# One-DMA loads for q, k and a, a removed pair of tiles, and 28 unread products behind TensorE's first fillers, in a fused gated-attention and feed-forward kernel

## The chip, the cores and the metric

The kernel runs on one core of a Trainium2 chip. The metric is the device time of one execution in microseconds (us). Before the change, three runs took 514.45, 516.45 and 517.21 us, with a median of 516.45 us. Lower is better.

A core has five engines that run side by side and wait for each other by semaphores: TensorE (PE, matrix products; its weight loads are shown apart as PEld), VectorE (DVE), ScalarE (ACT), GpSimd (POOL) and SyncE (SP), which here only issues DMAs. SBUF is the on-chip memory with 128 rows, PSUM the accumulator of TensorE.

## The reference

A gated linear recurrence for 4 batches of 8 heads, 768 tokens, 48 values a head, followed by a feed-forward block with an ELU on 3072 tokens:

```
for t in range(S):
    state = alpha[:, :, t, :, None] * state + np.einsum('bhd,bhe->bhde', k[:, :, t], v[:, :, t])
    y[:, :, t] = np.einsum('bhd,bhde->bhe', q[:, :, t], state)
...
h = x @ w_in                                          # 3072x384 by 384x2048
g = np.where(h > 0.0, h, np.exp(np.minimum(h, 0.0)) - 1.0)
return g @ w_out                                      # 3072x2048 by 2048x384
```

## The kernel before

The work falls into a recurrence part and a feed-forward part, in one stream of instructions for each engine.

**Recurrence.** The 768 tokens of each batch are cut into 6 chunks of 128 tokens, so there are 24 chunks, numbered i. (The title of the code's list is `win`; here they are called chunks, since "window" is a view of the profile.) Heads go in pairs: a pair has one head in rows 0 to 47 of SBUF and the other in rows 64 to 111; rows 48 to 63 and 112 to 127 are padding. For each chunk, `SC` takes running products of a (alpha) on VectorE, `LN` and `EX` take logarithm and exponential on ScalarE, `KA`, `KB`, `KC` and `SQ` scale k and q by them, `TP` transposes k on TensorE and `KN` copies the result (later chunks do it in `TA`, `TB` and `T` on VectorE), `S` makes the scores k by q, `MK` masks them, `U` makes k by v, `UP`, `UA`, `UB` and `UC` carry the state on, and `YL`, `Y3`, `Y`, `XH`, `XP` and `XL` make the output y and split it into a rounded upper and a remaining lower part, the input of the feed-forward part.

**Feed-forward.** 3072 tokens are 12 blocks of 256, and the 2048 hidden values are 8 slices of 256. For block b and slice j, `A` is 18 products of 128x256 (h), `RA`, `RB`, `RC`, `GH` and `GL` apply the ELU and split it, and `O` is 12 products of 128x384. The weights come as 16 loads of 768 KB (`F.0` to `F.15`); `DA`, `DB` and `DC` on VectorE, `WH` on ScalarE and `WP` or `WL` on TensorE, ScalarE, GpSimd or VectorE turn them into the upper and lower parts that TensorE uses.

**Order.** Each engine's order is written out by hand: the text `START` lists steps as name and number (`L.3` is step `L` for chunk 3), and `STEADY` does the same for the rest. Every step issues its instructions in that order, on whatever engines it uses, and each engine takes its own in order. All loads before the last block go through one queue, SP's. In the part that matters here the order on SP is

```
LA.0 LA.1 LB.0 LB.1 F.0 F.2 LV.0 LV.1 LV.2 L.2 L.3 F.4 F.6 LV.3 F.12 F.3 F.1 F.7 L.4 LV.5 F.5 L.5 F.11 F.10 F.9 F.14 LV.4 F.8 L.7 L.6
```

`LV` loads v. `LA` and `LB` load a and then k and q of chunks 0 and 1, over all 128 rows. `L` (line 178) loads all three of a later chunk into one of `NQ` = 3 tiles `qka`: for chunk 2 in one DMA over 128 rows (770 KB), and from chunk 3 on in two DMAs of 48 rows (289 KB each), without the padding rows. A load of chunk i has to wait until the last reader of chunk i - 3 is done with the tile; for `L.3` that is `S.0`.

**The head of the program.** `first` is a constant of 1e-30 with ones in some places, set by VectorE. As soon as it is there, TensorE runs `X(WARM)`: 12 products of 128x512 on it, read as bf16 and written to the PSUM tile `wp`, which nobody reads. They are here called the fillers. Next on TensorE stands `TP.0` (line 285), which waits for `KC.0` on VectorE (line 244). GpSimd meanwhile sets constants and clears parts of the v tiles (line 135) and two tiles `v0` (line 139); step `V0`, which would load them, stands in no list, and `U` reads them in no chunk.

Of the kernel before, what the change touches and what calls it, by code (L numbers as in the profile page):

```python
# [8 lines left out]
F32 = mybir.dt.float32  # L9
F32R = mybir.dt.float32r  # L10
# [4 lines left out]
B, H, S, D = 4, 8, 768, 48  # L15
# [11 lines left out]
QW = 2 * NP * W + NP * AW  # L27
# [3 lines left out]
EARLY = 6  # L31
# [3 lines left out]
QU, QS = 6, 6  # L35
# [53 lines left out]
def gla_elu_ffn(ctx: ExitStack, tc: tile.TileContext, qka, vv, vn, wgt, out):  # L89
    nc = tc.nc  # L90

    const = ctx.enter_context(tc.tile_pool(name="const", bufs=1))
    weights = ctx.enter_context(tc.tile_pool(name="weights", bufs=1))
    main = ctx.enter_context(ExitStack())
    work = main.enter_context(tc.tile_pool(name="work", bufs=2))
# [10 lines left out]
    for a in range(2):  # L106
        nc.vector.tensor_copy(out=sel[64 * a:64 * a + 64, a, :, D:64],
                              in_=ident[64 * a:64 * a + 64, 64 * a:64 * a + D].rearrange("p (x c) -> p c x", c=NC))
# [4 lines left out]
    for h0 in (0, 64):  # L113

        nc.gpsimd.affine_select(
            out=mask[h0:h0 + 64, :], in_=mask[h0:h0 + 64, :], pattern=[[1, C]],
            compare_op=ALU.is_ge, fill=0.0, base=0, channel_multiplier=-1)
    first = const.tile([128, NP, AW], F32, name="first")
    nc.vector.memset(first, 1e-30)
    nc.vector.memset(first[:, :, 0:1], 1.0)  # L120
    wp = psa.tile([128, 512], F32, name="wp", tag="pa")
    wz = first.rearrange("p n w -> p (n w)").bitcast(mybir.dt.bfloat16)

    def X(n):
        for _ in range(n):
            nc.tensor.matmul(wp, lhsT=wz[:, 0:128], rhs=wz[:, 0:512], start=True, stop=True)

    X(WARM)

    NB = 4  # L130

    HD = 2 * NP * D
    vs_t = [work.tile([128, 3 * HD + 16], F32, name=f"vs{i}", tag=f"vs{i}", bufs=1) for i in range(NB)]
    for t in vs_t:
        nc.gpsimd.memset(t[:, 2 * HD:], 0.0)

    v0 = [work.tile([128, HD], F32, name=f"v0{i}", tag=f"v0{i}", bufs=1) for i in range(2)]
    for t in v0:
        nc.gpsimd.memset(t, 0.0)

    def lhs(i, c, a):

# [23 lines left out]
    NQ = 3  # L166
    qka_t = [work.tile([128, QW], F32, name=f"qka{i}", tag=f"qka{i}", bufs=1) for i in range(NQ)]

    def qtile(i):
        t = win[i]["t"] = qka_t[i % NQ]  # L170
        return t


    @tok
    def L(i):
        t = qtile(i)
        for r in [slice(0, 128)] if i < NQ else [slice(0, D), slice(64, 64 + D)]:
            nc.sync.dma_start(out=t[r], in_=qka[i, r, 0:QW])

    @tok  # L180
    def LA(i):
# [14 lines left out]
            nc.sync.dma_start(out=vs[0:64, 0:2 * HD], in_=vv[i, 0:64])  # L196
            nc.sync.dma_start(out=vs[64:128, HD:3 * HD], in_=vv[i, 64:128])


    @tok  # L200
    def V0(i):
        if EARLY <= i < QU:
            nc.sync.dma_start(out=v0[i % 2][0:64], in_=vv[i, 0:64, HD:2 * HD])

    @tok
    def SC(i):
# [548 lines left out]
    start = [t.split(".") for t in START.split()]  # L755
# [215 lines left out]
```

## Time and profile before

| | before |
|---|---|
| runs | 514.45, 516.45, 517.21 us (median 516.45) |
| profiled execution, span | 516.5 us |
| PE busy | 501.1 us (97%) |
| DVE busy | 391.1 us (76%) |
| ACT busy | 288.9 us (56%) |
| POOL busy | 127.9 us (25%) |
| DMA queue of SP | 55.69 MB, 38.0% of 16 engines' span |
| mean granted TensorE clock | 0.978 |

The span runs from the first to the last instruction of the profiled execution; it has no other time beside it, and it agrees with the median of the runs. Idle time of an engine is shown in front of the instruction that ended it, with the one that released it ("<-"). The granted clock (PEclk) is a share of TensorE's full speed. The DMA share is the mean busy share of the 16 DMA engines.

### The profile page before, as it was taken

To read this page: it belongs to the slowest core of one execution; us is meant where nothing else is said; L and a number is where in the kernel's file an instruction comes from. 1 tells how busy PE (TensorE), PEld (TensorE's weight loads), DVE (VectorE), ACT (ScalarE), POOL (GpSimd) and SP (SyncE) were. 2 spreads that over 40 slices of the span, in tenths; PEclk is the share of its full clock that TensorE was granted. 3 is DMA by queue.
4 is the path that set the end of the run, shared out by engine and by line. 5 is a ranking of instruction groups with operands and counts; after the bars stand their busy time and mean duration, and the time that the engine had idled before them with its cause. 6 is when DMAs were issued, how large, how long until landed. Compare 5 with 4: busy or idle time off the path is not lost.

```text
span 516.5 us, 13313 instructions
## 1 busy us (share of the span) xinstructions
PE 501.1 (97%) x5400; PEld 484.2 (94%) x5400; DVE 391.1 (76%) x808; ACT 288.9 (56%) x689; POOL 127.9 (25%) x110
## 2 busy tenths in 40 slices
PE   5998999998999999999999999999999999999995
PEld 2887999997999999999999999999999999999995
DVE  7886999997989878886986987886987987244321
ACT  3463667544564366755755655756655656454432
POOL 2020855463213300501511511501501500000000
PEclk8698999998999999999999999999999999999999
DMA  8999724217221426326326326326323321210001
GB/s 303 322 314 313 210 58 155 75 41 161 67 75 27 68 94 162 93 72 160 97 73 160 92 79 154 93 83 148 94 87 99 93 66 44 62 39 10 2 32 36
DMA packets 22069, 57.00 MB, mean 110 GB/s; under 512 B 3217, under 2 KB 10129, under 8 KB 22001
## 3 DMA queue, kind: packets, MB, share of 16 engines
q1 hardware_dynamic: 21712, 55.69, 38.0%
q8 instruction: 44, 0.72, 0.6%
q10 hardware_dynamic: 288, 0.39, 0.2%
q14 instruction: 25, 0.20, 0.1%
HBM read 49.39 MB, written 4.72 MB: 105 GB/s over the span
## 4 chain that ended last, share of the span: by engine, by line
PE 85%; DMA 6%; DVE 4%; issue 2%; POOL 1%; ACT 1%; SPq 0%; DVEq 0%; POOLq 0%
PE o L709 39%; PE h L658 37%; DMA qka<-in_qka_dram 4%; PE y L461 4%; DMA raw<-in_wgt_dram 2%; PE q L377 2%; PE q L333 2%; PE y L456 1%; DVE st L361 1%; PE sc L349 1%; DVE P L212 0%; DVE kn L295 0%; DVE spare L596 0%; DVE spare L590 0%; DVE h L676 0%
## 5 line engine op out<-in xcount | busy, mean ns | idle before, releaser
L658 PE MATMUL h<-xt,w 128*128 128x256 f32 x1728 | 217.3, 283 | 1.9 <-DVE st L361 1.9
L658 PEld LDWEIGHTS h<-xt,w 128*128 128x128 f32 x1728 | 211.3, 190 | 4.0 <-issue 2.2
L709 PE MATMUL o<-w,gh 128*128 128x384 f32 x768 | 199.1, 340 | 0.0
L709 PEld LDWEIGHTS o<-w,gh 128*128 128x128 f32 x768 | 136.9, 188 | 0.8
L709 PE MATMUL o<-w,gl 128*128 128x384 f32 x384 | 130.0, 339 | 0.1
L682 ACT CAST gh<-h 128x512 fp32r<-128x512 f32 x96 | 56.0, 583 | 81.2 <-DVE h L676 44.4
L695 DVE TENSOR_TENSOR gl<-h,gh 128x512 fp32r<-128x512 f32 x96 | 65.9, 687 | 36.7 <-ACT gh L682 35.2
L295 DVE STREAM_TRANSPOSE kn<-qka 32x128 f32<-32x128 f32 x288 | 87.1, 303 | 4.5
L666 ACT ACTIVATE r<-h 128x512 f32<-128x512 f32 x96 | 56.9, 596 | 55.0 <-PE h L658 52.2
L676 DVE SCALAR_TENSOR_TENSOR h<-r,h 128x512 f32<-128x512 f32 x96 | 64.4, 688 | 15.4 <-ACT r L671 14.6
L709 PEld LDWEIGHTS o<-w,gl 128*128 128x128 f32 x384 | 72.1, 188 | 0.4 <-DVE gl L695 0.4
L234 POOL TENSOR_TENSOR qka<-qka,R 128x512 f32<-128x512 f32 x19 | 24.6, 1295 | 192.9 <-DVE gl L695 117.2
L671 ACT ACTIVATE r<-r 128x512 f32<-128x512 f32 x96 | 59.1, 632 | 0.6
L264 POOL TENSOR_TENSOR st<-qka,P 64x512 f32<-64x512 f32 x36 | 43.6, 1211 | 15.1 <-DVE P L212 13.3
L361 DVE TENSOR_TENSOR st<-q,mask 64x256 f32<-64x256 f32 x72 | 30.4, 422 | 10.8 <-ACT vs L412 9.2
L212 DVE TENSOR_TENSOR_SCAN P<-qka,first 128x516 f32<-128x516 f32 x24 | 30.2, 1264 | 3.4 <-DMA qka<-in_qka_dram 3.0
L239 POOL TENSOR_TENSOR R<-P,R 128x512 f32<-128x512 f32 x20 | 25.1, 1257 | 11.2 <-DVE qka L234 9.8
L221 ACT ACTIVATE R<-P 128x512 f32<-128x512 f32 x24 | 15.2, 633 | 22.6 <-DVE P L212 22.6
L414 DVE TENSOR_TENSOR vs<-vs,q 48x192 f32<-48x192 f32 x30 | 10.5, 349 | 21.3 <-PE q L333 17.0
L514 ACT ACTIVATE y<-y 128x128 fp32r<-128x128 f32 x20 | 5.6, 278 | 29.7 <-PE y L461 27.5
L642 POOL TENSOR_TENSOR w<-spare,w 128x768 fp32r<-128x768 f32 x6 | 16.0, 2674 | 19.7 <-ACT w L622 19.6
L614 ACT ACTIVATE ck<-ck,lim 128x384 f32<-128x384 f32 x32 | 20.7, 646 | 0.1
(102 smaller groups left out, 438.5 us busy)
## 6 DMA issues: line engine op xcount, KB each, us to landing
raw<-in_wgt_dram SPq DMA_DIRECT2D x16, 768.0 KB, 13.1
ck<-in_wgt_dram SPq DMA_DIRECT2D x32, 384.0 KB, 3.1
qka<-in_qka_dram SPq DMA_DIRECT2D x42, 288.8 KB, 6.8
vs<-in_vv_dram SPq DMA_DIRECT2D x36, 192.0 KB, 3.9
out_dram<-ot SPq DMA_DIRECT2D x22, 192.0 KB, 1.9
vs<-in_vv_dram SPq DMA_DIRECT2D x6, 384.0 KB, 11.9
xt<-y SPq DMA_DIRECT2D x40, 48.0 KB, 2.3
qka<-in_qka_dram SPq DMA_DIRECT2D x2, 512.0 KB, 6.2
```

The costliest lines, as they stand in the source:

```text
L212: nc.vector.tensor_tensor_scan(out=P.rearrange("p n w -> p (n w)"), data0=t[:, 2 * NP * W:], data1=first.rearrange("p n w -> p (n w)"), in ...
L239: eng(KBV, i).tensor_tensor(out=d["R"], in0=pw(i), in1=d["R"], op=ALU.mult)
L264: eng(SQV, i).tensor_tensor(out=st[r, a], in0=d["q"][r], in1=pw(i)[r], op=ALU.mult)
L295: nc.vector.transpose(out=kn[32 * t:32 * t + 32, :, 32 * g:32 * g + 32], in_=d["kt"][32 * g:32 * g + 32, :, 32 * t:32 * t + 32])
L361: nc.vector.tensor_tensor(out=d["st"][r, a, :, c * C:(c + 1) * C], in0=d["s4"][a][o], in1=mask[o].unsqueeze(1).broadcast_to([64, NP, C]), ...
L658: nc.tensor.matmul(h[:, f, :], lhsT=t[:, wi, ws], rhs=x[:, c, xi, :], start=(f == 0 and k == 0), stop=(k == 8), skip_group_check=True)
L666: nc.scalar.activation(out=r, in_=d["h"], func=AF.Relu, scale=-1.0)
L671: nc.scalar.activation(out=d["r"], in_=d["r"], func=AF.Exp, scale=-1.0)
L676: nc.vector.scalar_tensor_tensor(out=d["h"], in0=d["r"], scalar=-1.0, in1=d["h"], op0=ALU.add, op1=ALU.max)
L682: nc.scalar.copy(out=gh, in_=d["h"])
L695: nc.vector.tensor_tensor(out=gl, in0=d["h"], in1=d["gh"].bitcast(F32), op=ALU.subtract)
L709: nc.tensor.matmul(o[:, 0:DM], lhsT=gt[:, f, ms], rhs=t[:, wi, f * DM:f * DM + DM], start=(j == 0 and f == 0 and k == 0), stop=(j == NJ - ...
```

## The change

Three edits. The first removes the two `v0` tiles, their two clears on GpSimd and the step that was never called. The second makes `L` one DMA over all 128 rows for every chunk, so the padding rows are loaded too. The third adds, behind the fillers, a constant `fr` (a copy of 512 columns of `first` on ScalarE, rounded to fp32r) and 28 products into `wp`, which nobody reads: 17 of 256 columns in fp32r (5 and 4 plain ones, 4 whose moving operand repeats one column, 4 over 64 rows), 8 of 256 columns in bf16, and 3 of 512 columns in fp32r.

```diff
     X(WARM)
+    fr = const.tile([128, 512], F32R, name="fr")
+    nc.scalar.copy(out=fr, in_=first.rearrange("p n w -> p (n w)")[:, 0:512])
+
+    def probe(n, w, lhs, rhs, start):
+        for _ in range(n):
+            nc.tensor.matmul(wp[:, 0:w], lhsT=lhs, rhs=rhs, start=start, stop=True, skip_group_check=True)
+
+    probe(5, 256, fr[:, 0:128], fr[:, 0:256], True)
+    probe(4, 256, fr[:, 0:128], fr[:, 0:256], False)
+    probe(4, 256, wz[:, 0:128], wz[:, 0:256], False)
+    probe(4, 256, wz[:, 0:128], wz[:, 0:256], True)
+    probe(4, 256, fr[:, 0:128], fr[:, 0:1].broadcast_to([128, 256]), False)
+    probe(4, 256, fr[0:64, 0:128], fr[0:64, 0:256], False)
+    probe(3, 512, fr[:, 0:128], fr[:, 0:512], False)
...
-    v0 = [work.tile([128, HD], F32, name=f"v0{i}", tag=f"v0{i}", bufs=1) for i in range(2)]
-    for t in v0:
-        nc.gpsimd.memset(t, 0.0)
...
     def L(i):
         t = qtile(i)
-        for r in [slice(0, 128)] if i < NQ else [slice(0, D), slice(64, 64 + D)]:
-            nc.sync.dma_start(out=t[r], in_=qka[i, r, 0:QW])
+        nc.sync.dma_start(out=t, in_=qka[i, :, 0:QW])
...
-    @tok
-    def V0(i):
-        if EARLY <= i < QU:
-            nc.sync.dma_start(out=v0[i % 2][0:64], in_=vv[i, 0:64, HD:2 * HD])
```

The order changes at two places. The first is TensorE's, at the end of the fillers (`wp` from `first`) and the start of chunk 0 (`tp`, `sc`). Before:

```order
L126 LDWEIGHTS first
L126 MATMUL wp<-first 128x512
L285 MATMUL tp<-ident,qka_123 128x128 x4
L349 MATMUL sc<-st,qka_123 64x64 x16
L285 MATMUL tp<-ident,qka_124 128x128 x4
```

With the change (of eight like pairs on `first`, one is shown):

```order
L126 LDWEIGHTS first
L126 MATMUL wp<-first 128x512
L134 MATMUL wp<-fr 128x256 x9
L134 LDWEIGHTS first
L134 MATMUL wp<-first 128x256
...
L134 MATMUL wp<-fr 128x256 x8
L134 MATMUL wp<-fr 128x512 x3
L289 MATMUL tp<-ident,qka_149 128x128 x4
L353 MATMUL sc<-st,qka_149 64x64 x16
```

So 28 products now stand between the last filler and the transposes of chunk 0; nothing else on TensorE moves.

The second place is SP's queue from `L.2` (the first row) to `L.4`; `qka` are the tiles of the loads in question, `raw` weights, `vs` v. Before:

```order
L178 DMA qka_125<-in_qka_dram 128x1540
L178 DMA qka_123<-in_qka_dram 48x1540 x2
L568 DMA raw_235<-in_wgt_dram 128x1536 x2
L194 DMA vs_108<-in_vv_dram 128x768
L568 DMA raw_294<-in_wgt_dram 128x1536
L568 DMA raw_328<-in_wgt_dram 128x1536 x2
L568 DMA raw_378<-in_wgt_dram 128x1536
L178 DMA qka_124<-in_qka_dram 48x1540 x2
```

With the change:

```order
L187 DMA qka_151<-in_qka_dram 128x1540
L187 DMA qka_149<-in_qka_dram 128x1540
L572 DMA raw_260<-in_wgt_dram 128x1536 x2
L203 DMA vs_138<-in_vv_dram 128x768
L572 DMA raw_319<-in_wgt_dram 128x1536
L572 DMA raw_353<-in_wgt_dram 128x1536 x2
L572 DMA raw_403<-in_wgt_dram 128x1536
L187 DMA qka_150<-in_qka_dram 128x1540
```

The sequence of loads stays; each of the loads of chunk 3 and later is one issue of 128 rows in place of two of 48.

## The prediction

> **What bounds the kernel now.** I read the page's engine lines first, then TensorE's waits, then stretches of the first 54 us, and last single rows of them.
>
> ```profile
> PE 501.1 (97%) x5400; PEld 484.2 (94%) x5400; DVE 391.1 (76%) x808; ACT 288.9 (56%) x689; POOL 127.9 (25%) x110
> PEclk8698999998999999999999999999999999999999
> DMA  8999724217221426326326326326323321210001
> ```
>
> TensorE is busy for 501.1 of 516.5 us, so an edit counts only if it removes TensorE's idle time or lets it run faster. The other two lines give each fortieth of the span: the clock is low in the second slice (12.9 to 25.8 us), and the DMA engines are full in the first four.
>
> ```profile
> PE tp L285 <- DVE qka L244: 3.6, 1, 3.6
> PE yl L456 <- DVE vs L414: 2.1, 1, 2.1
> PE h L658 <- DVE st L361: 1.9, 1, 1.9
> ```
>
> These are TensorE's waits (us in total, times, longest) apart from 2.1 us at the very start: one behind the fillers, one near 45 us, one near 123 us. The next view gives stretches: start and end, length, busy time (and count) of PE, PEld, DVE, ACT and POOL, then granted clock, DMA share and GB/s.
>
> ```profile
> 6.24:9.66 3.42, 0.49 (x3) 0.00 (x0) 1.99 (x4) 1.25 (x4) 0.00 (x0) 0.95 1.01 392
> 9.66:13.07 3.41, 2.71 (x36) 2.41 (x36) 3.34 (x6) 0.72 (x2) 0.00 (x0) 0.50 1.01 414
> 13.07:16.48 3.41, 3.41 (x48) 2.84 (x44) 3.34 (x3) 1.68 (x5) 0.00 (x0) 0.50 1.09 378
> 16.48:19.90 3.42, 3.42 (x60) 3.15 (x60) 1.74 (x3) 1.05 (x2) 0.00 (x0) 0.50 1.00 184
> 19.90:23.31 3.41, 3.41 (x18) 2.73 (x16) 3.12 (x5) 0.85 (x2) 1.18 (x1) 0.55 0.99 338
> 23.31:26.72 3.41, 3.41 (x71) 2.64 (x71) 2.46 (x4) 2.48 (x8) 0.00 (x0) 1.00 1.01 407
> 43.79:47.20 3.41, 1.26 (x17) 1.06 (x15) 2.29 (x4) 0.60 (x1) 0.00 (x0) 0.95 0.98 288
> 47.20:50.61 3.41, 3.41 (x54) 2.96 (x53) 3.38 (x3) 1.61 (x4) 0.00 (x0) 0.54 1.00 399
> ```
>
> Each of the waits is followed by half clock. TensorE works only 0.49 us of 6.24:9.66, and then runs at 0.50 from 9.66 to about 23.3 us; it works 1.26 us of 43.79:47.20, and runs at half for the next 3.4 us. So from 10.4 to 23.3 us TensorE is "busy" all the time because it is slow.
>
> ```profile
> 8.00:16.00 8.00, 5.64 (x72) 4.89 (x72) 7.83 (x11) 2.29 (x6) 0.00 (x0) 0.58 1.04 408
> 16.00:20.00 4.00, 4.00 (x68) 3.61 (x65) 2.32 (x3) 1.16 (x3) 0.00 (x0) 0.50 1.04 188
> 24.00:32.00 8.00, 8.00 (x150) 6.60 (x148) 6.75 (x9) 5.10 (x15) 0.00 (x0) 1.00 1.03 416
> 34.00:46.00 12.00, 10.64 (x147) 9.81 (x143) 6.87 (x10) 5.93 (x12) 3.86 (x2) 1.00 1.02 238
> 124.00:128.00 4.00, 2.87 (x14) 2.90 (x15) 1.67 (x4) 0.00 (x0) 3.48 (x3) 0.68 1.02 182
> ```
>
> The DMA engines are full in all five, yet move 408 to 416 GB/s in some and 182 to 238 in others. What differs is what is under way, by SP's issues:
>
> ```profile
> 6.04 8.14 SPq L178 DMA_DIRECT2D qka<-in_qka_dram  x3
> 121.85 2.46 SPq L178 DMA_DIRECT2D qka<-in_qka_dram  x4
> ```
>
> The three issues from 6.04 us are `L.2` and the two halves of `L.3`, the last of them about 14.2 us, and 16:20 is slow; behind 34:46 stand the halves of `L.4` and `L.5`; and 124:128 holds hardly anything but the four halves issued from 121.85 us. `L.2`, with rows just as long but 128 of them, lies in the fast 8:16. So the loads of 48 rows halve the rate, of everything beside them too.
>
> **The change, part by part: the probes.** I call the 28 new products probes. They have 25 x 256 + 3 x 512 = 7,936 columns.
>
> ```profile
> 2.08 4.65 PE L126 MATMUL wp<-first 128*128 128x512 bf16 x12 [2.08 <-DVE first L120]
> 10.36 1.08 PE L285 MATMUL tp<-ident,qka 128*128 128x128 f32 x4 [3.63 <-DVE qka L244]
> 4.62 0.15 PEld L126 LDWEIGHTS <-first 128*128 128x128 bf16 x1 [0.27 <-issue]
> 5.04 0.15 PEld L126 LDWEIGHTS <-first 128*128 128x128 bf16 x1 [0.28 <-issue]
> 69.92 2.12 PE h L658 x18
> 72.04 4.24 PE o L709 x24
> ```
>
> The last two are pieces of the chain that ended last: 18 products of 256 columns in 2.12 us (0.118 each), 24 of 384 in 4.24 (0.46 ns a column). At this rate the probes take 25 x 0.118 + 3 x 0.236 = 3.66 us, and the hole from 6.73 to 10.36 us is 3.63. I cost them at 0.03 us, hidden by the wait for `KC.0`. Fillers come every 0.42 us (4.62 to 5.04), 512 columns at half of that rate, although the clock column starts at 1.00; at that rate the probes would take 6.5 us and `TP.0` would be 2.9 us late. The forms that no row shows (a repeated column, 64 rows, adding onto `wp`) I put between these two ends and take the faster, as the nearest row, `h`, is the same fp32r at 256 columns. The copy to `fr` lies on ScalarE, idle from 2.1 to 4.87 us.
>
> What they buy is the clock, if a TensorE that doesn't pause keeps 1.00 beyond 9.66 us. Then the work of 10.4 to 23.3 us shrinks to about half, but what TensorE does there depends on VectorE, which has no gap from 7.6 to 17.4 us. So I add up the waits that fall away on VectorE and ScalarE:
>
> ```profile
> 18.39 0.36 DVE L445 SCALAR_TENSOR_TENSOR vs<-u,P 128x192 f32<-128x192 f32 x1 [1.02 <-PE u L395]
> 19.41 1.23 DVE L212 TENSOR_TENSOR_SCAN P<-qka,first 128x516 f32<-128x516 f32 x1 [0.66 <-DMA qka<-in_qka_dram]
> 22.07 0.36 DVE L445 SCALAR_TENSOR_TENSOR vs<-u,P 128x192 f32<-128x192 f32 x1 [0.25 <-PE u L421]
> 24.77 0.27 ACT L489 COPY y<-yl 128x128 f32<-128x128 f32 x1 [0.70 <-PE yl L456]
> ```
>
> 1.02 and 0.25 (for `U.0` and `UP.1` on TensorE), 0.66 (the landing of `L.2`, whose tail shares 16:20 with `L.3`) and 0.70 (`YL.0`) lie one behind the other on the way to `Y.0`: 2.63 us. `Y.0` starts at 25.13 us now and would start near 22.5; what is late next there is ScalarE's `LN.2` and `EX.2`. TensorE's 13.0 us at half clock would be 6.5 at full, of which 2.6 come out at `Y.0`; the other 3.9 us become holes in front of it.
>
> **The loads.** Of one chunk 591 KB become 788 KB. The next rows say what waits for them.
>
> ```profile
> 40.21 1.23 DVE L212 TENSOR_TENSOR_SCAN P<-qka,first 128x516 f32<-128x516 f32 x1 [1.59 <-DMA qka<-in_qka_dram]
> 44.91 0.96 DVE L584 TENSOR_SCALAR wm<-raw 128x1536 int32<-128x1536 int32 x1 [3.46 <-DMA raw<-in_wgt_dram]
> 46.38 0.35 DVE L414 TENSOR_TENSOR vs<-vs,u 128x192 f32<-128x192 f32 x1
> 46.78 1.11 PE L456 MATMUL yl<-st,vs 48*64 48x64 f32 x16 [2.15 <-DVE vs L414]
> 47.82 1.55 PE L500 MATMUL y<-y,sel 128*64 128x128 f32 x12
> 51.29 0.88 PE L500 MATMUL y<-y,sel 128*64 128x128 f32 x12
> ```
>
> VectorE waits for `L.4`, then for the weights `F.5` that queue behind it; its step at 46.38 us then ends TensorE's wait of 2.15 us. At 408 GB/s, 16:20 would take 4.0 x 188/408 = 1.84 us, and 34 to 44.9 would take 10.9 x 238/408 = 6.4: 6.7 us less. The added padding of `L.3` and `L.4` costs 2 x 197 KB / 408 GB/s = 1.0. `F.5` lands 5.7 us earlier, near 39.2; VectorE is there by then (2.6 us earlier than now, and without the 1.59).
>
> TensorE is without a gap from 25.13 to 44.64 us at clock 1.00, so it brings its 2.6 us to 42.0. The row of 46.38 us comes 5.7 earlier, at 40.7, and the wait of 2.15 us is gone. With it goes the half clock of 47.20:50.61: `Y.2` from 47.82 takes 3.47 us, the same work for chunk 3 from 51.29 to 53.62 at full clock 2.33, and some 0.2 more for `YL.3`: 1.35 us.
>
> From there to 123 us TensorE has no wait; VectorE, full until 92 us, is 5.7 or more ahead of now, near TensorE's 6.1, and sets the rest by at most 0.4. The third wait (1.9 us at 123 us) hangs on a chain that starts from TensorE itself, and I leave it. Dropping `v0` frees GpSimd at 3.6 us, where nobody waits for it: nothing.
>
> **The sum:** 2.6 + 2.15 + 1.35 = 6.1 us, less 0.03 for the probes: **516.5 - 6.0 = 510.5 us.** The span agrees with the median of the runs (516.45), so it needs no correction.
>
> The Trainium skill speaks against the second part: "DMA: Bandwidth & Descriptors", section "Why a DMA increments its semaphore by 16 and not by 1", says that 48 rows are split over 16 engines just as 128 are, so that only bytes would count. By it the larger loads would cost 197 KB more each and win nothing, 517.5 in all (the mild form of the last rival below); the trace disagrees, with 182 GB/s at a full DMA share against 408. For the clock, "TensorE: Matmul & The Clock Gate", section "Part 1: The HAM clock gate", lets one busy stretch of 3.4 us restore full speed. The trace agrees for 47.20:50.61, but not for 9.66 to 23.31 us, four stretches of which three are wholly busy; by the rule alone the first rival below would hardly have a chance.
>
> **The rivals.**
>
> *The clock falls anyway.* That three busy stretches of transposes, scores and k by v did not bring it back says that this work hardly counts as activity, so it may not hold it either. For holding it: from 23.31 us on, similarly small products (71 in 3.41 us) run at 1.00. Then the 2.6 us fall away: 516.5 - 2.15 - 1.35 = 513.0.
>
> *The probes run at half clock*, since the clock may rise at another moment in another execution: `TP.0` up to 2.9 us late. From 10.36 us to the end of `U.0` at about 18.3 TensorE takes 7.9 us at half clock, at full clock with its holes some 5.6 (an estimate), so `U.0` would end near 16.0, 1.4 us before VectorE is free for it. So 1.5 us of the gain go, and at most all 2.6: 512.0 to 513.0.
>
> *The loads give nothing that TensorE sees:* `F.5` is less than 4.8 us earlier and the wait is shortened only, or another engine takes its place. 514 to 516.5.
>
> *Slower:* the rate isn't a matter of rows, and the larger loads run at 188 to 238 GB/s as now. Then `L.3` and `L.4` carry 394 KB more in front of `F.5`, 1.7 to 2.1 us; VectorE's row at 44.91 and TensorE's at 46.78 come that much later, and a faster clock before only lengthens the wait: 518.4. (In a mild form, where the slow stretches have another cause and the added bytes go at 408 GB/s, it is 1.0 us: 517.5, no change.) It decides once the rate gains less than the bytes, a third. Against it: `L.2`.
>
> **How the numbers follow.** The forecast has 0.60, and with the smaller terms' spread it reaches from 508 to 512 (lower by 1.7 if the half clock behind 123 us, which needs a pause at one moment, doesn't come: 507.5 as the lower end). The clock rival has 0.17, the half-clock probes 0.08, the hidden loads 0.10, the slower one 0.05. A measurement of this kernel tells about 0.5% (2.6 us) from no change. Forecast and the first two rivals are faster than 513.9, bar a few hundredths: 0.81 faster, 0.14 same, 0.05 slower. The range from 507.5 to 514.0 leaves out the last two rivals and little else.
>
> **What would show it.** Right: the probes end near 10.4 us, TensorE's clock stays 1.00 through 10 to 23 us, `Y.0` starts near 22.5, no stretch before 56 us with a full DMA share moves under 350 GB/s, `F.5` has no waiter, and the wait near 45 us and the half clock behind it are gone. Wrong: 0.50 in 10 to 23 us (then 513); a hole of 3 us that has only moved to 15 or 40 us; loads of 128 rows near 200 GB/s; or a new wait of TensorE for VectorE between 54 and 66 us, where VectorE is full.

## The result and the profile after

The kernel with the change took 508.14 us (median of four runs, 507.37 to 510.17), the kernel before 515.78 us (four runs, 514.45 to 517.21) on the same chip: a ratio of 0.9847 with a 95% interval of 0.9814 to 0.9879, 7.6 us less. The forecast was 510.5 us, and its range of 507.5 to 514.0 us held the time, 0.6 us from its lower end. Each ratio below is to the kernel before in the same set of runs (medians 515.9, 517.1 and 516.8 us in the three sets of experiments; two runs of 604 and 1013 us in the second are not counted). The profiled execution of the change has a span of 505.7 us, against 516.5 before.

TensorE's waits after the change (what waits and for whom; us in total, times, longest):

```profile
PE wp L126 <- DVE first L120: 2.1, 1, 2.1
PE h L662 <- DMA xt<-y: 1.3, 1, 1.3
PE y L504 <- ACT y L493: 0.7, 1, 0.7
PE u L399 <- ACT kn L318: 0.7, 1, 0.7
PE u L425 <- DVE vs L449: 0.4, 1, 0.4
```

The waits of 3.6 us behind the fillers and of 2.1 us near 45 us are gone. The third is shorter and has another name here (a DMA in place of VectorE). Three small ones are new; they are the holes in front of `Y.0`. The same stretches as before, with the columns start and end, length, busy time of PE, PEld, DVE, ACT and POOL, granted clock, DMA share and GB/s:

```profile
6.27:10.42 4.15, 4.15 (x30) 3.58 (x29) 2.83 (x5) 1.31 (x4) 0.00 (x0) 1.00 0.99 390
10.42:22.17 11.75, 9.73 (x176) 7.74 (x174) 11.09 (x14) 5.23 (x14) 1.18 (x1) 1.00 1.02 415
16.00:20.00 4.00, 3.58 (x42) 2.70 (x42) 3.91 (x6) 1.05 (x2) 1.03 (x1) 1.00 1.01 407
24.00:32.00 8.00, 8.00 (x151) 6.76 (x146) 7.74 (x9) 4.63 (x14) 0.00 (x0) 1.00 1.02 413
34.00:46.00 12.00, 12.00 (x230) 11.03 (x231) 11.51 (x16) 6.78 (x16) 4.68 (x3) 1.00 1.02 413
```

The clock is 1.00 throughout. Before, it was 0.50 from 9.35 to 23.00 us (the prediction's stretches were cut 0.3 us later than the clock's own steps):

```profile
9.35:23.00 13.65, 12.64 (x143) 10.84 (x143) 11.51 (x15) 3.99 (x10) 1.18 (x1) 0.50 1.03 329
```

16:20 moves 407 GB/s in place of 188, and 34:46 moves 413 in place of 238. Single rows of TensorE, in order of time (start, us):

```profile
8.34 2.25 PE L134 MATMUL wp<-fr 128*128 128x256 f32 x11
10.42 0.60 PE L289 MATMUL tp<-ident,qka 128*128 128x128 f32 x4
22.17 0.88 PE L504 MATMUL y<-y,sel 128*64 128x128 f32 x12 [0.69 <-ACT y L493]
41.45 0.73 PE L460 MATMUL yl<-st,vs 48*64 48x64 f32 x16
46.78 2.41 PE L662 MATMUL h<-xt,w 128*128 128x256 f32 x18
117.15 2.37 PE L662 MATMUL h<-xt,w 128*128 128x256 f32 x18 [1.31 <-DMA xt<-y]
```

The first row holds the last eleven probes. The other five instructions stood before at 10.36, 25.13, 46.78, 53.62 and 125.13 us, so they come 0.06 later, then 2.96, 5.33, 6.84 and 7.98 earlier. And VectorE has the chunk's a and the weights when it comes to them:

```profile
35.85 1.23 DVE L216 TENSOR_TENSOR_SCAN P<-qka,first 128x516 f32<-128x516 f32 x1 [0.20 <-POOL w L646]
37.00 0.93 DVE L588 TENSOR_SCALAR wm<-raw 128x1536 int32<-128x1536 int32 x1
```

No DMA ended an idle time there; before, these rows stood at 40.21 and 44.91 us, behind waits for DMA of 1.59 and 3.46 us.

### The profile page after: what moved, and what is told of

Its sections match the earlier page's. It is cut to its first block, busy times and chain, and to the rows that moved or that the text cites. A ratio compares the mean times of both kernels' runs of the same rounds, so it can differ in the third digit from the quotient of the medians.

```text
span 505.7 us, 13302 instructions
## 1 busy us (share of the span) xinstructions
PE 495.8 (98%) x5428; PEld 480.1 (95%) x5428; DVE 391.2 (77%) x808; ACT 289.6 (57%) x690; POOL 129.2 (26%) x108
## 4 chain that ended last, share of the span: by engine, by line
PE 93%; DVE 2%; DMA 2%; ACT 1%; SPq 1%; issue 0%; DVEq 0%
PE h L662 41%; PE o L713 40%; PE y L465 4%; PE y L460 2%; PE q L381 2%; PE q L337 2%; DMA qka<-in_qka_dram 1%; PE sc L353 1%; PE u L399 1%; DMA xt<-y 1%; PE y L504 1%; DVE wm L594 0%; DVE wm L600 0%; PE tp L289 0%; DVE qka L238 0%
## 5 line engine op out<-in xcount | busy, mean ns | idle before, releaser
L365 DVE TENSOR_TENSOR st<-q,mask 64x256 f32<-64x256 f32 x72 | 30.4, 422 | 10.8 <-ACT vs L416 9.2
```

Of the source, the lines that this page charges most:

```text
L365: nc.vector.tensor_tensor(out=d["st"][r, a, :, c * C:(c + 1) * C], in0=d["s4"][a][o], in1=mask[o].unsqueeze(1).broadcast_to([64, NP, C]), ...
```

## The experiments

Theory: the 3.6 us pause and the loads are two legs. The clock alone only brings TensorE sooner to a wait for weights; the loads alone leave TensorE at half clock. Rivals: one leg does it all, or the gains add. The first set (the probes alone, the loads alone, two of 64 rows, plain fillers) has 23 runs of the kernel before; the third set is half as many fillers, the two tiles, and two of the three kernels on the third wait; all else is in the second.

**Probes alone.** The change with the loads of before:

```diff
-        nc.sync.dma_start(out=t, in_=qka[i, :, 0:QW])
+        for r in [slice(0, 128)] if i < NQ else [slice(0, D), slice(64, 64 + D)]:
+            nc.sync.dma_start(out=t[r], in_=qka[i, r, 0:QW])
```

> The kernel with the change, but with the loads of before (two of 48 rows for each chunk from 3 on). Theory (two legs): TensorE runs at 1.00 from 10 to 23 us and is some 2 us early at Y.0, but VectorE still waits for F.5 until near 44 us, because the DMA engines are full at 190 to 240 GB/s; so TensorE's wait near 45 us grows from 2.15 to 4 us or more, half clock follows, and the time is within 1 us of before (ratio 0.998 to 1.002). Rival (the clock does it all, the loads were hidden): about 508, ratio 0.985, no long wait near 45 us. Rival (the gains simply add): 2.6 us, ratio 0.995.

Measured: 515.63 us, ratio 1.0001 (0.9979 to 1.0024). Its longest wait of TensorE, then stretches (columns as above), then TensorE's `TP.0` and `Y.0` and VectorE's row:

```profile
PE yl L461 <- DVE vs L419: 5.0, 1, 5.0
```

```profile
14.53:17.95 3.42, 2.73 (x73) 2.38 (x68) 2.56 (x3) 1.56 (x5) 0.00 (x0) 1.00 1.06 266
17.95:21.36 3.41, 3.41 (x8) 2.52 (x9) 2.79 (x5) 0.49 (x2) 1.18 (x1) 0.50 0.98 260
34.00:44.00 10.00, 8.35 (x125) 7.65 (x123) 6.10 (x7) 4.16 (x10) 2.99 (x2) 1.00 1.02 218
47.36:52.00 4.64, 4.64 (x67) 4.19 (x69) 4.61 (x3) 1.60 (x4) 0.00 (x0) 0.50 1.01 410
```

```profile
11.38 0.60 PE L290 MATMUL tp<-ident,qka 128*128 128x128 f32 x4
23.00 0.88 PE L505 MATMUL y<-y,sel 128*64 128x128 f32 x12
45.48 0.96 DVE L589 TENSOR_SCALAR wm<-raw 128x1536 int32<-128x1536 int32 x1 [4.08 <-DMA raw<-in_wgt_dram]
```

As the theory has it: TensorE is 2.1 us early at `Y.0` (23.00), then waits 5.0 us for VectorE, which waits for weights to 45.48 us, and 4.64 us at half clock follow. "The clock does it all" and "the gains add" fall. Two rivals of the prediction show up here in part. The clock did fall once in the small products, at 17.95 us for 3.41 us, though TensorE was busy for 2.73 of the 3.42 us before. And the fillers ran slow for longer: the probes began at 6.82 us instead of 6.27 and `TP.0` at 11.38, which is 1.65 us after `KC.0` had ended (9.04 + 0.69). Neither came like this in the two traces of the change.

**Loads alone.** The same line the other way round, in the kernel before.

> The kernel before with the loads over 128 rows in one DMA, nothing else. Theory (two legs): the granted clock is 0.50 from about 10 to 23 us as before, TensorE has no wait near 45 us and no half clock behind it, Y.0 starts near 25 us; 2.15 + 1.35 us, perhaps 1 more from the wait near 123 us: 3.5 to 5 us less than before, ratio 0.990 to 0.993. Rival (the loads do it all): 508, ratio 0.985. Rival (the clock does it all): ratio 0.998 to 1.002. DMA in 34 to 44 us: over 400 GB/s by the theory, 190 to 240 if the rate is not a matter of rows.

Measured: 510.63 us, ratio 0.9905 (0.9879 to 0.9931). Two stretches:

```profile
10.66:24.32 13.66, 13.66 (x146) 11.55 (x146) 11.15 (x14) 5.03 (x12) 1.18 (x1) 0.51 1.02 414
34.00:44.00 10.00, 10.00 (x161) 9.45 (x157) 9.55 (x12) 5.48 (x12) 4.41 (x2) 1.00 0.94 354
```

Half clock as before, no wait near 45 us. The DMA engines are no longer full all the time in 34:44 (0.94); their share dips to 0.5 and 0.8 only in 35 to 37 us, while at a full share they move 369 to 430 GB/s. So the loads are worth 5 us, the probes 0 without them, and 2.5 us more with them (the change took 508.1 us, its variant with plain fillers 508.2 in this set, against 510.6).

**Why the larger loads are faster: 64 rows twice, and 112 rows.** Both on the kernel with the change; the removed line stands in both edits, the first two added lines are the edit for two of 64 rows, the last two that for 112:

```diff
-        nc.sync.dma_start(out=t, in_=qka[i, :, 0:QW])
+        for r in [slice(0, 128)] if i < NQ else [slice(0, 64), slice(64, 128)]:
+            nc.sync.dma_start(out=t[r], in_=qka[i, r, 0:QW])
+        n = 128 if i < NQ else 112
+        nc.sync.dma_start(out=t[0:n], in_=qka[i, 0:n, 0:QW])
```

> The kernel with the change, but each load from chunk 3 on as two DMAs of 64 rows (0 to 63 and 64 to 127): the same 788 KB, twice the issues. Theory (the rate goes with the rows that one DMA covers): 64 of 128 rows give half of 410 GB/s, so about 205 to 240 GB/s at a full DMA share while they run, F.5 lands at 45 us or later, the wait near 45 us is back: ratio 0.998 to 1.006. Rival (it is the shape of 48 rows, three for each of 16 engines, or their odd bounds): over 400 GB/s and the time of the change, ratio 0.985. Rival (it is the second issue for each load): like the theory in time, but with a full rate in between.

> The kernel with the change, with each load from chunk 3 on over rows 0 to 111 in one DMA (690 KB; the last 16 padding rows are left out). Theory (the rate goes with the rows covered): 112 of 128 rows give about 360 GB/s while they run, the same time for a load as 128 rows; VectorE has no wait for F.5 in the change, so the same time as the change, ratio 0.982 to 0.988. Rival (only 128 rows run at full rate, anything less at half): 690 KB at 200 GB/s, F.5 near 45 us, the wait near 45 us is back, ratio about 1.0.

Measured: two of 64 rows 519.62 us, ratio 1.0073 (1.0046 to 1.0101); 112 rows 513.64 us, ratio 0.9945 (0.9917 to 0.9973). Stretches of the one:

```profile
16.00:20.00 4.00, 3.58 (x48) 2.82 (x44) 2.44 (x3) 1.05 (x2) 0.00 (x0) 1.00 1.02 224
34.00:44.00 10.00, 9.16 (x132) 8.47 (x130) 4.84 (x7) 4.01 (x9) 4.22 (x2) 1.00 1.02 228
```

and of the other, with TensorE's wait:

```profile
16.00:20.00 4.00, 3.36 (x34) 2.31 (x30) 3.10 (x5) 1.05 (x2) 0.60 (x1) 1.00 1.02 246
32.00:36.00 4.00, 4.00 (x57) 3.77 (x56) 3.17 (x2) 3.34 (x6) 1.86 (x1) 1.00 1.02 247
```

```profile
PE yl L461 <- DVE vs L419: 3.6, 1, 3.6
```

These are rates of stretches, with loads of weights beside the loads in question. The same bytes in two DMAs of 64 rows run at 224 to 228 GB/s, so the rate is set neither by bytes nor by the odd 48. It is not the number of issues alone either: 112 rows are one DMA and run at 246 in these stretches (281 over 34:44), not at the 360 that rows in proportion would give. Only with the full 128 rows did the stretches run at 407 to 413. My rule "the rate goes with the rows" falls; what holds is that 48, 64 and 112 rows all ran far below 128. Why, no run here shows; 112 was not tried further.

**The form of the products.** The 28 products and `fr` replaced:

```diff
-    probe(5, 256, fr[:, 0:128], fr[:, 0:256], True)
...
+    X(17)
```

> The kernel with the change, but with 17 more plain bf16 fillers of 512 columns in place of the 28 products of several forms (and without fr). 17 x 0.216 us are 3.7 us at full clock, as long as the 28. Theory (only that TensorE does not pause counts, not the form): the last filler ends near 10.4 us, clock 1.00 through 10 to 23 us, ratio 0.983 to 0.988. Rival (fp32r products or the mix keep the clock up, bf16 fillers do not): 0.50 behind 10 us, and the time of the loads alone, ratio about 0.991.

Measured: 508.17 us, ratio 0.9859 (0.983 to 0.9887), with full clock:

```profile
10.00:23.00 13.00, 10.97 (x186) 8.49 (x185) 12.34 (x15) 5.55 (x15) 1.19 (x1) 1.00 1.02 415
```

The form does not matter; the theory holds.

**The change again, and its products twice.** The second kernel repeats the block of seven `probe` lines.

> The kernel with the change, unaltered, beside the others of this set. Any theory: ratio 0.982 to 0.988 of before.

> The kernel with the change, with the 28 products run twice: 3.7 us more on TensorE, of which none is hidden by the wait for KC.0. The holes of TensorE in front of Y.0 (about 2 us) can take a part. By the forecast's working 1.5 to 2.6 us later than the change, ratio to before 0.988 to 0.991. Rival (the early stretch is not critical once the loads are fast): the time of the change. Rival (nothing takes it up): 3.7 us later, ratio 0.992.

Measured: the change 507.73 us, ratio 0.9826 (0.9786 to 0.9866); products twice 510.38 us, ratio 0.987 (0.9828 to 0.9912). With the products twice:

```profile
15.45 0.60 PE L296 MATMUL tp<-ident,qka 128*128 128x128 f32 x4
```

`TP.0` is 5.0 us later than in the change's trace (the fillers there were late too), the time 2.65 us later. The cover is used up, and about half of what is over is taken up behind it, where TensorE has 2.0 us of holes in front of `Y.0` (11.75 - 9.73 in the stretch from 10.42 us). The 2.65 us lie just above the worked-out 1.5 to 2.6.

**Half as many fillers.** `X(8)` in place of `X(17)`.

> The kernel with the change, with 8 plain bf16 fillers of 512 columns in place of the 28 products: they end near 8.5 us and TensorE pauses some 1.9 us before the transposes of chunk 0. Theory (a pause of the order of the waits near 45 and 123 us, 2.15 and 1.94 us, is enough): clock 0.50 from about 10 to 23 us, and the time of the loads alone, ratio about 0.990. Rival (only a pause near a whole stretch of 3.4 us does it): clock 1.00 and the time of the change, ratio 0.983 to 0.986. Between: it depends on where the pause falls in the free-running stretches, and the runs differ among themselves by more than 2 us.

Measured: 508.66 us, ratio 0.9853 (0.9813 to 0.9892), runs from 507.18 to 510.14. In the profiled execution the pause was short, since the transposes were ready sooner:

```profile
2.08 6.83 PE L126 MATMUL wp<-first 128*128 128x512 bf16 x20 [2.08 <-DVE first L120]
9.38 0.63 PE L276 MATMUL tp<-ident,qka 128*128 128x128 f32 x4 [0.47 <-issue]
```

So fewer do nearly as well, but the pause looked at was 0.47 us, not the 1.9 that I had meant to set. The slowest run, 510.14 us, had a mean granted clock of 0.989, the fastest 1.000; the loads alone had 0.983 to 0.987. So in some executions the clock may have fallen after all; no trace shows one.

How long a pause may be can be read from all traces together. In each, the steps of the clock lie whole multiples of 3.413 us apart: before, at 9.35, 23.00, 46.89, 50.31, 125.40 and 128.81 us. Cut on that grid, stretches with little work of TensorE look so (three of the kernel before, one of it without `v0`, one of the change):

```profile
5.93:9.35 3.42, 0.80 (x4) 0.19 (x2) 1.74 (x4) 1.56 (x5) 0.00 (x0) 1.00 1.00 381
43.48:46.89 3.41, 1.26 (x12) 1.06 (x13) 1.98 (x4) 0.60 (x1) 0.00 (x0) 1.00 1.00 277
121.99:125.40 3.41, 1.47 (x9) 1.18 (x8) 3.29 (x8) 1.09 (x4) 2.64 (x3) 1.00 0.79 181
119.91:123.32 3.41, 1.74 (x15) 1.77 (x15) 2.29 (x5) 0.00 (x0) 3.26 (x4) 1.00 0.88 201
114.94:118.35 3.41, 2.10 (x16) 1.81 (x15) 3.25 (x7) 0.70 (x4) 2.68 (x3) 1.00 0.91 266
```

The clock fell behind the first three and held behind the last two. Apart from the very end of the program it fell ten times in the 14 traces: nine times behind a stretch with 1.47 us of work or less, and once, with the probes alone, behind one with 2.73. It held behind every stretch with 1.74 us or more but that one, some with the same 2.73. So a pause matters by how much work it leaves in its stretch: one of 1.94 us cost the clock before, one of 1.84 us did not without `v0`. Why the stretch of 2.73 us lost it stays open.

**The two tiles.** The kernel before without `v0` and its clears.

> The kernel before without the two v0 tiles and their clears on GpSimd, nothing else. Every theory: no change, ratio 0.997 to 1.003; GpSimd is free at 3.6 us instead of 4.4, and its next instruction waits until 20.7 us.

Measured: 515.61 us, ratio 0.9978 (0.9951 to 1.0004): no change that could be told from none. What the removal does is free two tiles of 384 values a row in SBUF (3 KB), of which `fr` takes 512 values (2 KB).

**The third wait.** The prediction had left it out as a chain through `MK` on VectorE. In the trace of the change it has the name of a DMA; in that of the change run again it has VectorE's name once more:

```profile
PE h L662 <- DVE st L365: 1.4, 1, 1.4
```

So the name alone decides nothing. SP's queue in the change (start, us until the last issue):

```profile
110.40 0.83 SPq L724 DMA_DIRECT2D out_dram<-ot  x2
111.28 0.47 SPq L205 DMA_DIRECT2D vs<-in_vv_dram  x1
111.80 0.60 SPq L206 DMA_DIRECT2D vs<-in_vv_dram  x1
112.50 1.31 SPq L552 DMA_DIRECT2D xt<-y  x2
```

The last two issues are `XD.5`; its data are ready at 106 us (`XL.5` on VectorE), but it stands behind the outputs `Z.0`, which wait for ScalarE. The edit moves one name in `START`, here in the change and in the kernel before (and, as a last kernel, together with the plain fillers):

```diff
-O.0.7 XL.5 UC.6 LV.9 TB.7 ... MK.6 XD.5 A.2.1
+O.0.7 XL.5 UC.6 LV.9 XD.5 TB.7 ... MK.6 A.2.1
```

> The kernel with the change, with the two small DMAs of step XD.5 (the rows of the last head pair of chunk 5 into xt) moved in SP's queue in front of Z.0's outputs and LV.8, behind LV.9. In the change they are ready at 106 us but issued at 112.5, land at 116.9 and TensorE waits 1.3 us for them. Theory: the wait of A.2.1 goes, 1.0 to 1.3 us less than the change, ratio to before 0.980 to 0.985. Rival (MK.6 on VectorE or a PSUM tile is late next): same time as the change.

> The kernel before with only the two small DMAs of step XD.5 moved in SP's queue behind LV.9, in front of Z.0's outputs. Theory (the third wait near 123 us is for these DMAs, not for MK on VectorE as the waits name it): the wait of 1.9 us goes, and with it the half clock behind it in the executions that have it: 2 to 3.5 us less than before, ratio 0.993 to 0.996. Rival (the wait is for MK.6 or MK.7 on VectorE): no change, ratio 0.998 to 1.002, and the wait is still there.

> The kernel with the change, with 17 plain bf16 fillers in place of the 28 products and with XD.5's DMAs moved: the two variants that were as fast as the change or faster, together. Theory: the time of the moved DMAs alone, ratio 0.979 to 0.983.

Measured: on the change 506.54 us, ratio 0.9804 (0.9763 to 0.9845); on the kernel before 515.06 us, ratio 0.9969 (0.9942 to 0.9997); with the plain fillers 506.62 us, ratio 0.9802 (0.9763 to 0.9841). TensorE's longest waits with the edit on the change; there `A.2.1` on TensorE and `MK.6` on VectorE (four instructions); and `A.2.1` with the edit on the kernel before:

```profile
PE wp L126 <- DVE first L120: 2.1, 1, 2.1
PE y L504 <- ACT y L493: 0.7, 1, 0.7
PE u L399 <- ACT kn L318: 0.7, 1, 0.7
```

```profile
115.22 2.28 PE L662 MATMUL h<-xt,w 128*128 128x256 f32 x18
115.56 1.75 DVE L365 TENSOR_TENSOR st<-q,mask 64x256 f32<-64x256 f32 x4
```

```profile
121.99 2.28 PE L658 MATMUL h<-xt,w 128*128 128x256 f32 x18
```

In both the wait is gone: the last has no idle time in front of it. In the first, `MK.6` ends at 117.31 us, 2.1 us after `A.2.1` has begun (115.22), so it cannot have been what was waited for. The gain on the kernel before is 1.6 us, less than the 2 to 3.5 us that I expected; on the change it is 1.2 us, with runs that overlap a little (505.37 to 507.38 against 506.89 to 508.34). The two versions with both, at 506.5 and 506.6 us, are the fastest of all.

## Why the prediction was right, step by step

- **The bound.** TensorE's pauses, the half clock behind them and the DMA rate were where the time lay. The two legs together gave 7.6 us, and neither alone did. The prediction's prices for one leg alone can be read from its rivals: with the loads hidden 514 to 516.5 us, and the probes alone took 515.63; with the clock down 513.0, and the loads alone took 510.63, 2.4 us less. So the leg of the loads was priced too low, mostly behind 54 us (the sixth point): in its trace the `h` of 53.62 us comes 3.3 us earlier, near the 3.5 of the sum.
- **The probes' cost: 0.03 us worked out, 0.06 measured** (`TP.0` at 10.42 against 10.36). The fp32r products of 256 columns went at the rate taken from `h`; the last 11, with repeated column, 64 rows or 512 columns, took 2.08 us where the rate gives 8 x 0.118 + 3 x 0.236 = 1.65. That was the form without a row, and its excess lay under the cover. That 0.06 comes so near is luck of this pair of traces: the end of `KC.0` and that of the probes both move from one execution to the next. `TP.0` starts 0.10 us after `KC.0` ends before, 0.24 with the change, 0.60 with the change run again, and 1.65 with the probes alone.
- **`Y.0`: 2.6 us worked out, 2.96 measured.** The clock stayed, VectorE's waits of 1.02, 0.66 and 0.25 went, and ScalarE is late next, as forecast (TensorE's wait of 0.69 us at `Y.0`). The holes in front of `Y.0` were put at 3.9 us and are 2.0: TensorE's work there, 14.77 us before, shrank to 9.73 and not to 8.3 (an estimate: 13.0 us halved, and the rest).
- **The wait near 45 us: 2.15 worked out, 5.33 - 2.96 = 2.37 measured.** The loads' rate was foreseen at 408 GB/s and came at 407 to 413. The argument against it in the prediction, that only bytes should count, falls with the two DMAs of 64 rows: the same bytes at 224 to 228 GB/s.
- **The half clock behind it: 1.35 worked out, 6.84 - 5.33 = 1.51 measured.**
- **After 54 us: nothing up to 0.4 worked out, more measured.** Up to the third wait TensorE won another 0.5 us (7.35 at its start). The step that failed is "hangs on a chain that starts from TensorE itself, and I leave it". The wait was for `XD.5`'s DMAs, which had the loads of 48 rows right behind them in the queue. With the change it is 1.31 in place of 1.94 us, and no half clock follows: the next `h` comes at 120.06 instead of 129.56 us, 9.5 earlier. In the pair of traces this is 2.2 us that the sum lacks. The prediction had the missing half clock as a possibility of 1.7 us for its lower end, though its 507.5 is not what that gives (508 - 1.7 = 506.3). Whether it comes is no effect of the edit alone: without `v0` the wait was 1.84 us and the clock held.
- **Span and median: "needs no correction" was wrong.** In the change's runs the time is 1.7 us more than the span (507.37 with 505.7, 510.17 with 508.5), so by the same difference the profiled execution before stands for about 518.2 us, 2.4 above the median of 515.8. Traces of nearly the same kernel show how it varies: the wait near 45 us was 2.15 us in its trace, 0.5 in that with only `XD.5` moved, and absent in that without `v0`. So the traces differ by 10.8 us and the medians by 7.6; the forecast of 6.0 is short of both.
- **The rivals.** "Slower" and "hidden loads" fell with 413 GB/s and no waiter for `F.5`. The half-clock probes exist: where the fillers came 0.43 us apart until 6.7 us (the probes alone, the products twice) in place of 5.5, the first probes ran slow too. The traces of the change don't have it; its runs, from 507.4 to 510.2 us, don't rule it out for single executions. The falling clock was seen once, with the probes alone.

## What to carry to other kernels

A wait has to be followed past the first engine that ends it: filling TensorE's pause was worth nothing until the DMAs behind the next wait were faster, and then 2.5 us. Compare GB/s at a full DMA share between stretches, and look for the load that halves it; here loading useless padding rows made everything beside it faster. Where a wait is put down to an engine's step that ends about when a DMA lands, move the DMA before believing it. And to keep the clock, a pause need not be filled whole: here 8 fillers did nearly as well as 28 products.

## What the runs showed of the hardware that I had not expected

- At a full DMA share, stretches with loads of rows just as long, beside loads of weights, moved 407 to 413 GB/s with 128 rows in one DMA, 246 to 281 with 112 rows, 224 to 228 with two DMAs of 64 rows, and 182 to 278 with two of 48.
- The granted clock changed only at multiples of 3.413 us within a trace. It fell behind stretches of that length with at most 1.47 us of TensorE's work, and held from 1.74 us up, but for one stretch with 2.73.
- Work does not always bring it back: it stayed at 0.50 for 13.65 us, four such stretches, in all four traces with the early pause, though TensorE was busy all the time in the last three of them.
- The last 11 probes took a quarter longer than the rate of `h` gives, but not because of their forms: within a form, starts were 0.11 to 0.12 us apart for 256 columns, 64 rows included; around each change of form single starts came 0.08 to 0.11 us later than that.
